# A gated linear attention and a maxout FFN: attention output computed with features on the rows, and smaller tiles for scores and state sums

## The chip, the cores and the metric

The kernel runs on one core of a Trainium2 chip. The metric is the device time of one execution in microseconds. Where a profile is quoted, its times are of one profiled execution: the span is the time from its first to its last instruction, and the execution's own time is a little longer. Engines are named as in the profile: PE (matrix products; PEld is its loading of the stationary operand), DVE, ACT and POOL (elementwise work), SP (issues transfers). Results of PE land in psum, which has eight banks here.

## What is computed

Four arrays q, k, v and alpha of 4 batches, 8 heads, 768 positions and 48 features. For each batch and head a 48 by 48 state runs over the positions, and its read-out goes through an FFN with a maximum over three products:

```
for t in range(S):
    state = alpha[:, :, t, :, None] * state + einsum('bhd,bhe->bhde', k[:, :, t], v[:, :, t])
    y[:, :, t] = einsum('bhd,bhde->bhe', q[:, :, t], state)
x = y.transpose(0, 2, 1, 3).reshape(B * S, H * D)              # 3072 x 384
out = max(max(x @ w1, x @ w2), x @ w3) @ w_out                 # 384 -> 768 -> 384
```

## The kernel before

**Groups and units.** The 768 positions of a batch are cut into chunks of 128. A group `n` is one batch and two neighbouring chunks, 256 positions, so there are 12 groups. On the 128 rows of the loaded tiles stand pairs of positions: rows 0 to 63 are chunk `i` = 0, rows 64 to 127 chunk `i` = 1, and the parity `r` of the position is an index beside the features. The eight heads of a group are two units `u` of four heads (`hh`); four heads are two pairs `j` of two heads `p`, and a pair of heads is padded to 2 x 64 features.

**Steps of a group.** The names are those of the steps in the code.

- `load`: transfers issued by SP. `aa`, `la` (POOL, DVE, ACT): products and logarithms of alpha. `Lp` (PE, L389), `L0` (DVE), `exp` (ACT, L398): prefix sums of the logarithms and their exponentials `ep` and `en`. `hp` (PE, L344), `e` and `G`: decays of whole chunks.
- `qk` (POOL or DVE, L403): q times `ep`, k times `en`, as 16-bit tiles. `v` (POOL or ACT): v scaled by `vsc`, a factor of the row.
- `tp` (PE, L421), `qkT` (DVE, L429): 16 transposes for a unit and their copy out of psum, so that features stand on the rows.
- `A` (PE, L441), `LA` (DVE, L449): scores of key against query, 16 matmuls for a unit with 48 rows by 64 stationary columns and 128 moving ones, and the causal mask. Keys stand on the rows of `LA`, queries in its columns.
- `pp` (PE, L472): state sums, k against v, for each chunk that a later one needs; 16 matmuls a group (8 in the last chunk pairs) with 64 rows by 128 stationary columns (two heads) and 96 moving ones. The off-diagonal blocks of the two heads are computed as well and not used. `add`, `Z`, `Zp` (DVE, POOL): the carried state, kept as a 16-bit tile `Z` with zero blocks between the heads.
- `yi` (PE, L509): output from the state, four matmuls a chunk with the queries `qkT` stationary, 128 by 128, and 96 columns of `Z` moving. `ya` (PE, L531): output from the chunk itself, 32 matmuls a group, `LA` stationary (64 by 128) and 48 columns of v moving, added to the same bank. The result `yp` has positions on the rows.
- `xb` (ACT or DVE, L247 and L249): `yp` out of psum, times `ysc`, a factor of the row. `xp` (PE, L551): three matmuls a chunk with `xb` stationary and a constant 0/1 matrix `order` moving, which put features on the rows and the positions back in their order. `xT` (DVE or ACT, L243): the copy out of psum.
- The FFN of a group: `gp` (PE, L575, six matmuls for each of six pieces of w2 - w1 and w3 - w1), `h0` and `h1` (ACT, DVE), `op` (PE, L603 and L606), `ob` (ACT, DVE) and `out` (SP). `d` (DVE, L281) makes the weight differences; `wt` and `mp` (L294, L307) make the product of w1 and w_out that carries the bypass.

**What sets the order.** Nothing is scheduled at run time. `ORDER` is a list written out ahead: each token is a step's number, the engine that runs it and the psum bank or banks that it gets (`17P0`: step 17 on PE with bank 0). `Plan.emit` (L100) issues the steps in that order, so every engine works through its own part of the list in order, and waits where a step needs another engine's result or a bank or tile that is still in use. Weights are loaded by transfers that POOL issues (L272) between its other work, activations by SP (L262).

Of the kernel before, what the change touches and what calls it, by code (L numbers as in the profile page):

```python
# [10 lines left out]
FP32 = mybir.dt.float32  # L11
# [7 lines left out]
CDEC = 0.92  # L19
# [7 lines left out]
6S 0S 3S 1S 2S 52S 5S 7S 8V 9A 4S 10A 11G 17P0 54S 18V 13A 53S 19A 14P1 98S 28P2 12A 20A 55S 29V  # L27
15A 22V 100S 30A 31A 21V 99S 56V 101S 24P3 16G 143S 58A 32V 145S 57A 33V 74P5 144S 59P6 25V 62P7
35P0 146S 23A 63V 205S 26P2 64A 36V 272S 65A 34A 206S 75V 37P0 67G 27V 207S 60A 40P47 77A 274S 76A
61G 339S 66V 208S 42V 78G 69P2 38V 273S 39G 79V 41V 73G 81P5 68A 102G 82V 70V 83P0 80G 104A 44P4  # L30
85G 84V 86P56 45P2 87V 71P0 88V 46A 119P3 72V 103A 47P5 90P2 49A 120V 91P4 122A 193P0 92V 95A 105P1
121A 89V 108P4 93P2 48A 43V 96P3 50P6 123V 51A 94A 124V 109V 126P5 111A 97A 195P7 189V 106A 187V
196A 262P2 127V 321P3 194A 188V 128P5 110A 113V 254P1 112G 129V 258P7 255A 130G 329P0 115P4 192V
330A 197P1 107G 116V 114A 125G 331P6 198A 190V 117P4 325P0 322A 118V 147G 148A 256P1 191V 149A
131P34 263A 257V 153P5 259A 264P2 154V 133V 326A 132V 164P1 260P7 156A 265V 327P0 165V 261V 167A
135P3 323P2 166A 332V 155A 136P7 324V 169G 201P1 140V 158G 150P6 199P5 202A 137A 157V 151A 168V
160P2 328V 171P6 203P1 159A 170G 172V 200A 161V 173P6 204A 175P05 209G 174V 162P2 333P1 211A 163V
276G 277A 210A 218P6 269P7 334A 152G 219V 539S 278A 176V 275S 134V 221A 340S 177V 220A 141P2 229P3
138P1 341S 285P4 222G 230V 179P0 139A 266P6 142V 406S 231A 286V 342S 232A 223V 288A 234G 279P1
180P2 270A 267V 287A 212P3 178V 392P7 181A 233V 213A 296P6 225P4 280A 215G 184A 297V 236P2 290G  # L40
394P1 226V 299A 298A 237V 301G 182P0 393A 388P4 183V 344A 185P5 343G 238P2 395V 224A 227P6 336P0
186A 228V 289G 235A 389A 214G 239V 217G 390P1 337A 216G 345A 292P5 338S 300G 240P74 473S 293V 363P0
352P2 396P3 408S 353V 241V 474S 354A 463P5 391V 397A 268S 242G 398P6 335S 291A 282G 243V 409S 461P7
464A 281G 364V 302G 407S 399V 366A 459P3 284G 271S 365A 244V 476S 245P1 355A 246P5 460V 307P60 671S
357G 247P 462V 605S 294P2 251A 465P4 283G 295V 248A 356G 252P7 411A 455P5 253A 308V 368G 457P1 456A
466V 249P2 359P6 410G 458V 250A 303P3 346P5 529P2 304V 310G 412A 525P1 360V 309G 347A 530A 367G
305P3 311V 369A 361P5 521P7 306V 526A 349G 350G 358A 312P2 523P0 351G 522A 362V 543G 313P1 413P3
419P4 430P7 314P 414A 431V 370P5 420V 433A 467P3 524V 315A 435G 371V 318A 421A 477G 372P0 422A
374P25 545A 470P6 436G 479A 375V 478A 348G 373V 376G 432A 379P4 434G 480P2 471A 403P7 468A 424V
377V 486P0 319P1 423G 404A 531P6 487V 378V 488A 405S 380P3 527P7 481A 532V 608S 320A 541S 489A 381P  # L50
609G 528V 544A 475S 426P1 437P5 382A 540S 415G 316P0 427V 503G 400P7 317A 438V 416G 385V 383P4
552P1 401V 386P2 384A 591P0 483V 387A 402S 553V 484G 428P5 672S 592A 439P3 675G 497P7 555A 655P2
440V 554A 425G 593P0 611A 485G 498V 589P1 500A 418V 429V 491G 546P3 499A 653P4 587P7 417G 654A 594V
441P56 547A 676A 490V 563P4 533P3 442V 588V 443G 444G 656V 661P0 534A 501G 564V 447P5 535S 663P7
590V 662A 606S 492G 677A 446P2 445V 657P3 674S 565A 502G 664V 542S 566A 493P0 448P 658V 472S 482G
556G 504P6 607S 494V 508P4 624A 469S 659P3 452A 449V 610A 618P0 505V 595P1 450P5 453P2 596V 597P6
451A 454A 509V 536P7 660V 511G 549G 619V 568G 598V 621A 506P1 495P4 620A 678P3 551G 537A 725P6 496V
569G 679A 538S 684P0 612P7 719P3 557G 673S 685V 507V 665P4 567G 550V 686A 629P5 695P1 548V 599P2
510V 613A 720A 681V 623V 666A 615V 683V 723P7 622G 696V 630V 698A 602P3 724V 631A 614G 558G 687A
726V 635A 688G 721P4 697A 600V 603A 512P7 700G 601S 513P0 722V 632A 625P1 667S 514P 604S 626V 699G  # L60
574P6 515A 559P3 570P1 518A 727P5 634G 571V 701A 519P7 575V 729P0 616G 728A 560V 577G 516P1 668P2
633G 517V 730V 520V 627P5 669A 572P3 689V 561P0 737P7 670S 617V 573V 731P2 738A 562V 741P7 732A
578P3 576V 745P4 742A 628V 690A 579P0 636P1 580P 637V 640P7 581A 691P5 584V 638P1 746A 582P3 692V
747P0 583A 641V 644P4 743P5 639V 642G 739P6 643G 680V 585P3 645P7 740V 702P1 586A 646P 682V 706P3
703V 647A 734P6 650A 748V 707V 744V 704P1 709G 693P3 759P7 708G 735V 694V 755P0 757P5 705V 711P6
752P3 710P4 761P1 753A 756A 754S 648P2 712P 760A 733S 651P3 649A 749P0 762V 652A 716V 713V 777P7
750A 763P2 751S 736S 717P1 714P3 781P6 718A 779P4 782V 765P0 715V 783P1 778V 799P6 764V 801P3 766V
800A 773P7 784V 775P2 758V 793P0 780V 797P6 774V 795P1 791P5 767P4 792V 802V 770P7 776V 768A 796V
769S 794V 785P5 798V 771V 803P3 786V 772S 787S 807P4 804P 808P 805V 788P2 809A 806S 810S 789A 790S
# [44 lines left out]
def kernel(  # L114
# [20 lines left out]
    DP = 64  # L135
    NP = H // 2
# [11 lines left out]
    rr = np.arange(P)  # L148
# [11 lines left out]
    d16_np = np.concatenate(  # L160
        [np.eye(P)] + masks + [turned[:, None] == rr[None, :]], axis=1).astype(np.float16)
    dec = CDEC ** (2.0 * pair - (HALF - 2.0))
    c32_np = np.stack(
        [np.concatenate([SIG / dec] * 2), np.concatenate([dec / SIG] * 2),
         np.full(P, HALF * np.log(CDEC))], axis=1
# [6 lines left out]
    d16 = sb.tile([P, 4 * P], FP16, name="d16")  # L172
    c32 = sb.tile([P, 3], FP32, name="c32")
    tri, hsel = c16[:, :P], c16[:, P:]
    ident, maskA, order = d16[:, :P], d16[:, P:3 * P], d16[:, 3 * P:]
    vsc, ysc, hbias = c32[:, 0:1], c32[:, 1:2], c32[:, 2:3]
# [16 lines left out]
    v16s = homes(NQ, [P, HH, 2, D], FP16, "v")  # L193
    qkTs = homes(NT_, [P, UB, 2, 2, P], FP16, "qkT")
    LAs = homes(NT_, [P, 2, 2, 2, P], FP16, "LA")
    xbs = homes(3, [P, DM], FP16, "xb")
# [16 lines left out]
    for t in qks:  # L213
        nc.vector.memset(t[:, :, :, :, D:], 0.0)
    for zz in Zs:
        for t in zz:
            nc.gpsimd.memset(t, 0.0)
# [20 lines left out]
    live = {}  # L238
    LEAD, SLOPE = 5.5, 1.9
    WAFTER = {2: (0,), 4: (1,), 7: (2,), 11: (3,)}  # L240
# [76 lines left out]
    def decay(n):  # L317
# [21 lines left out]
        key = ("hp", n)  # L339

        def totals(eng):
            live[key] = bank(key, [P, NP, 2 * UB], FP32)
            for j in range(NP):
                nc.tensor.matmul(live[key][:, j, :], la[:, 0, 2 * j:2 * j + 2, :], hsel,  # L344
                                 start=True, stop=True)

        plan.step("hp", "PE", 2 * n + 0.5, totals, banks=[key],
                  reads=[("la", n % 3, h, 0) for h in range(2)], writes=[key])
# [3 lines left out]
                                                   in_=live[key], func=AFT.Exp, bias=hbias,  # L352
# [27 lines left out]
    def prep(u):  # L380
# [4 lines left out]
        Lk, tk, Ak = ("Lp", u), ("tp", u), ("A", u)  # L385
# [5 lines left out]
        plan.step("Lp", "PE", u, cums, banks=[Lk], reads=[("la", n % 3, hh, 0)], writes=[Lk])  # L391
# [9 lines left out]
        for w, x, e in ((0, "q", ep), (1, "k", en)):  # L401
# [7 lines left out]
                  lambda eng: scaled(eng, v16, ld["v"][n % NL][:, hs], vsc),  # L409
                  reads=[("v", n % NL, hh)], writes=[("v16", u % NQ)])  # L410
        qkT, LA = qkTs[u % NT_], LAs[u % NT_]

        def trans(eng):
            live[tk] = banks2(tk, FP16)[:, :, :4 * P]
            for w in range(2):
                for j in range(2):
                    for r in range(2):
                        for i in range(UB):
                            rows = slice(i * HALF, (i + 1) * HALF)
                            at = (4 * w + 2 * j + r) * HALF  # L420
                            nc.tensor.transpose(live[tk][:, i, at:at + HALF],  # L421
                                                qk[rows, w, r, 2 * j:2 * j + 2, :],
                                                ident[rows, rows])

        plan.step("tp", "PE", u, trans, banks=[tk],
                  reads=[("qk", u % NQ, 0), ("qk", u % NQ, 1)],
                  writes=[tk])
        plan.step("qkT", "DVE", u,
                  lambda eng: nc.vector.tensor_copy(  # L429
                      out=qkT.rearrange("p i w j t -> p i (w j t)"), in_=live[tk]),  # L430
                  reads=[tk], writes=[("qkT", u % NT_)])

        def scores(eng):
            live[Ak] = banks2(Ak, FP32)
            for j in range(2):
                for r in range(2):
                    for i in range(UB):
# [237 lines left out]
```

## Time and profile before

| | us |
|---|---|
| median of 3 runs (151.91 to 154.11) | 153.44 |
| the profiled execution's own time | 153.0 |
| its span | 151.2 |
| first FFN matmul (L575) starts | 28.14 |
| last FFN matmul (L606) ends | 147.85 |

In a profile, "L441 PE MATMUL psum<-qkT 48*64 48x128 f16 x384" is the group of 384 matmuls of line 441 with a stationary tile of 48 rows by 64 columns and 128 moving columns. The chain of waits goes back from the last instruction to what released each; its pieces are given in order of time, with start and length in us, and a piece of PE lasts until the next begins. The slices are fortieths of the span, 3.78 us each, and their digits tenths of busy time. Matmuls are pipelined, so that the mean time of one in the groups (240 ns for L441) is its latency; what one costs is read from the lengths of whole pieces in the chain.

### The profile page before, as it was taken

Reading aid. Unit: us, or ns where it says so; the run is one execution under the profiler, and the core shown is the slowest. Engines: PE = TensorE matmul, PEld = TensorE weight load, DVE = VectorE, ACT = ScalarE, POOL = GpSimd, SP = SyncE. Lnnn points to the kernel's source line nnn. Section 1 sums busy time; section 2 is a strip of 40 time slices with the busy share of each in tenths; the row PEclk is TensorE's granted clock in tenths of the full one; section 3 lists DMA queues with packets and bytes.
Section 4 is the critical chain, followed back from the end, with each engine's and each line's share of the span. In section 5 each row is a group of like instructions: output and inputs, shape, how many; then the busy total and the mean of one; then the engine's idle time right before and its main releaser. Section 6 shows DMA issues by size and latency. Waiting matters only on the chain.

```text
span 151.2 us, 5265 instructions
## 1 busy us (share of the span) xinstructions
PE 133.5 (88%) x2220; PEld 102.4 (68%) x2220; DVE 120.7 (80%) x210; ACT 82.3 (54%) x185; POOL 69.3 (46%) x106
## 2 busy tenths in 40 slices
PE   0145498999999999999999999998999999999991
PEld 0133276677766778888677878766868877888660
DVE  3188988769999999999698998899899992395920
ACT  3467246829576996777967756536627305210111
POOL 8114920080390697798992865688800220000000
PEclk9999999999999999999999999999999999999999
DMA  5999999999999999999529929960410002300124
GB/s 127 273 261 261 266 213 211 240 249 221 279 260 262 262 252 261 282 310 270 114 59 259 290 60 259 255 191 0 160 56 0 4 4 81 127 4 0 52 104 156
DMA packets 55880, 26.45 MB, mean 175 GB/s; under 512 B 50737, under 2 KB 55857, under 8 KB 55857
## 3 DMA queue, kind: packets, MB, share of 16 engines
q1 hardware_dynamic: 53440, 23.60, 63.5%
q0 software_dynamic: 1984, 2.36, 9.0%
q8 instruction: 17, 0.28, 0.8%
q10 hardware_dynamic: 432, 0.17, 0.5%
q14 instruction: 7, 0.05, 0.1%
HBM read 23.76 MB, written 4.72 MB: 188 GB/s over the span
## 4 chain that ended last, share of the span: by engine, by line
PE 74%; DMA 11%; SPq 5%; DVE 3%; issue 3%; ACT 2%; POOL 1%; ACTq 0%; DVEq 0%; POOLq 0%
PE psum L575 31%; PE psum L606 14%; PE psum L603 7%; DMA wcat<-in_moe_w_dram 7%; SPq L262 5%; PE psum L441 4%; DMA qn<-in_q_dram 4%; PE psum L421 4%; PE psum L531 3%; PE psum L472 3%; PE psum L551 2%; PE psum L307 2%; PE psum L509 2%; PE psum L389 1%; DVE Z L373 1%
## 5 line engine op out<-in xcount | busy, mean ns | idle before, releaser
L575 PE MATMUL psum<-xT,wcat 128*128 128x256 f16 x432 | 55.3, 277 | 0.3 <-DVE wcat L281 0.3
L575 PEld LDWEIGHTS <-wcat 128*128 128x128 f16 x432 | 40.7, 99 | 6.6 <-DVE wcat L281 0.5
L449 DVE TENSOR_TENSOR LA<-psum,d 128x1024 f16<-128x1024 f32 x24 | 28.8, 1219 | 3.8 <-PE psum L441 2.6
L606 PE MATMUL psum<-wo,hT 128*128 128x384 f16 x144 | 27.3, 326 | 0.0
L591 DVE TENSOR_TENSOR hT<-psum,hT 128x512 f16<-128x512 f32 x36 | 23.8, 681 | 3.2 <-PE psum L531 2.8
L403 POOL TENSOR_TENSOR qk<-qn,ep 128x384 f16<-128x384 f32 x16 | 16.7, 1052 | 14.5 <-ACT ep L398 14.0
L243 ACT COPY ob<-psum 128x384 f32<-128x384 f32 x17 | 8.1, 484 | 24.7 <-PE psum L606 24.7
L403 POOL TENSOR_TENSOR qk<-kn,en 128x384 f16<-128x384 f32 x15 | 15.0, 1001 | 13.0 <-ACT en L398 8.5
L606 PEld LDWEIGHTS <-hT 128*128 128x128 f16 x144 | 14.1, 98 | 9.3
L584 ACT ACTIVATE hT<-psum 128x512 f16<-128x512 f32 x25 | 14.6, 600 | 8.1 <-PE psum L575 7.9
L429 DVE COPY qkT<-psum 128x1024 f16<-128x1024 f16 x24 | 16.0, 684 | 1.4 <-PE psum L421 1.1
L603 PE MATMUL psum<-past,xT 128*128 128x384 f16 x72 | 15.7, 327 | 0.0
L421 PE MATMUL psum<-d,qk 64*128 64x64 f16 x384 | 10.6, 200 | 5.2 <-DVE qk L403 4.0
L398 ACT ACTIVATE en<-psum 128x384 f32<-128x384 f32 x24 | 11.8, 496 | 5.3 <-DVE psum L393 4.1
L398 ACT ACTIVATE ep<-psum 128x384 f32<-128x384 f32 x24 | 11.7, 492 | 4.6 <-POOL qk L403 2.9
L373 POOL TENSOR_TENSOR Z<-U,G 48x192 f16<-48x192 f32 x12 | 6.0, 504 | 16.3 <-DVE U L486 15.8
L421 PEld LDWEIGHTS <-qk 64*128 64x128 f16 x384 | 8.1, 100 | 8.0 <-DVE qk L403 5.3
L243 ACT CAST xT<-psum 128x384 f16<-128x384 f32 x19 | 8.8, 483 | 6.0 <-PE psum L551 5.7
L324 POOL TENSOR_TENSOR aa<-an 128x384 f32<-128x384 f32 (+1 forms) x11 | 10.7, 972 | 2.6 <-DMA an<-in_alpha_dram 2.5
L247 ACT ACTIVATE xb<-psum,c 128x384 f16<-128x384 f32 x17 | 9.4, 580 | 4.2 <-PE psum L531 4.1
L586 DVE TENSOR_SCALAR hT<-psum 128x512 f16<-128x512 f32 x11 | 7.5, 686 | 4.4 <-PE psum L575 4.3
L247 ACT ACTIVATE v<-vn,c 128x384 f16<-128x384 f32 x14 | 8.6, 617 | 4.3 <-DMA vn<-in_v_dram 3.9
(54 smaller groups left out, 193.8 us busy)
## 6 DMA issues: line engine op xcount, KB each, us to landing
out_dram<-ob SPq DMA_DIRECT2D x24, 192.0 KB, 2.0
an<-in_alpha_dram SPq DMA_DIRECT2D x11, 384.0 KB, 6.1
kn<-in_k_dram SPq DMA_DIRECT2D x11, 384.0 KB, 5.9
qn<-in_q_dram SPq DMA_DIRECT2D x11, 384.0 KB, 6.5
vn<-in_v_dram SPq DMA_DIRECT2D x11, 384.0 KB, 6.1
wcat<-in_moe_w_dram POOLq DMA_DIRECT2D x2, 576.0 KB, 11.3
w1s<-in_moe_w_dram POOLq DMA_DIRECT2D x1, 576.0 KB, 8.0
wo<-in_moe_w_out_dram POOLq DMA_DIRECT2D x1, 576.0 KB, 7.6
```

The costliest lines, as they stand in the source:

```text
L243: (nc.scalar.copy if eng == "ACT" else nc.vector.tensor_copy)(out=out, in_=in_)
L247: nc.scalar.activation(out=out, in_=in_, func=AFT.Copy, scale=factor)
L398: lambda eng, t=t, sign=sign: nc.scalar.activation(out=t, in_=live[Lk], func=AFT.Exp, scale=sign),
L403: lambda eng, w=w, x=x, e=e: on[eng].tensor_mul(qk[:, w, :, :, :D].rearrange("p r h d -> p h r d"), ld[x][n % NL][:, hs], e),
L421: nc.tensor.transpose(live[tk][:, i, at:at + HALF], qk[rows, w, r, 2 * j:2 * j + 2, :], ident[rows, rows])
L429: lambda eng: nc.vector.tensor_copy(out=qkT.rearrange("p i w j t -> p i (w j t)"), in_=live[tk]),
L449: lambda eng: nc.vector.tensor_mul(LA.rearrange("p a j r t -> p (a j) (r t)"), live[Ak].rearrange("p a (j t) -> p (a j) t", j=2), maskA.un ...
L575: nc.tensor.matmul(live[gk][:, jj, :], wcat[:, kt, g, c0:c0 + P], xT[:, kt, :], start=(kt == 0), stop=(kt == NFT - 1))
L584: nc.scalar.activation(out=h, in_=live[gk], func=AFT.Relu)
L591: lambda eng, h=h, gk=gk: nc.vector.tensor_max(h, live[gk], h),
L603: nc.tensor.matmul(live[ok], xT[:, kt, i * P:(i + 1) * P], past[:, kt, :], start=(kt == 0), stop=False)
L606: nc.tensor.matmul(live[ok], hT[:, kt, i * P:(i + 1) * P], wo16[:, kt, :], start=False, stop=(kt == NJ - 1))
```

## The change

The output of attention is computed with features on the rows at once. The 384 features of a position are twelve pieces of 32; piece `f` goes to rows 32 * (f mod 4) and column block f // 4 of the bank, which is how `xT` has them.

- `yi`: pieces of 32 features of `Z` are stationary (128 by 32), the queries `qkT` move (128 columns); 12 matmuls a chunk for 4.
- `ya`: 32 features of v are stationary (64 by 32), the masked scores `LA` move (128 columns); 64 matmuls a group for 32. A piece of 32 features can span two heads, and then gets a product from each; for that v16 is padded to 64 features with zeros, by six POOL memsets at the start.
- `xb` and `xp` go, with the matrix `order` and the tiles `xb`. `xT` is now one DVE product for a chunk, out of psum, times `ysc`, which has become a factor of the column (a 128 by 128 constant); it also puts the two parities back in order, by an output with a stride of two elements.
- `A`: 32 matmuls a unit with 32 stationary columns for 16 with 64. `pp`: stationary pieces of 32 features of one head, and only that head's 48 columns of v moving; 64 (32) matmuls for 16 (8).
- Eight matmuls with a zero tile, one to each bank, open the program on PE.
- Steps change their numbers, and `ORDER` is a new list: engines and order of other steps differ too. Of the `qk` products 36 are on POOL and 12 on DVE (31 and 17 before), of the `Z` products 28 on POOL and 4 on DVE, not counting the 8 of `Zp` (23 and 9 before); `h0` is on ACT 27 times and on DVE 9 (25 and 11); `xT` is on DVE 24 times (5, and 19 on ACT). Two further modes (`merged`, `joined`) come with the code and are switched off (`TB, HB = 99, 99`).

At the start the new list has these orders (loads by array and group; 0a and 0b are the two halves of group 0):

```
SP before:   k0b a0a a0b q0a k0a a1 q0b v0b v0a k1 q1 a2 v1 k2 q2 v2 a3 k3 q3
SP after:    a0b a0a k0a q0a q0b a1 k0b v0a v0b a2 q1 k1 q2 v1 k2 a3 v2 q3 k3
POOL before: aa G qk(unit 2, k) G qk(unit 3, q) w1 w2 aa v w3 qk(unit 4, q) w_out
POOL after:  aa aa G G v aa qk(unit 2, q) qk(unit 3, q) w1 w2 w3 qk(unit 4, k) G qk(unit 4, q) qk(unit 5, q) qk(unit 5, k) w_out
PE before, ahead of the first gp: ... pp(1) ya(0) A(2) Lp xp yi(1) ya(1) wt hp Lp xp xp xp tp(5) wt
PE after, ahead of the first gp:  ... ya(0) A(3) pp(1) tp(4) A(2) yi(1) tp(5) wt ya(1) wt A(5) wt A(4) Lp
DVE before, ahead of d: ... LA(2) L0 xb add add qk(5) qk(5) L0
DVE after, ahead of d:  ... add xT(0) xT(0) LA(2) qkT(5) qkT(4) xT(1) xT(1)
```

The diff, without the order list, the two modes that are switched off, and the declarations (`QD`, `AW` and `KW` are 32):

```diff
+    for t in v16s:
+        nc.gpsimd.memset(t[:, :, :, D:], 0.0)
...
         def scores(eng):
...
-                    for i in range(UB):
+                    for s0 in range(0, P, AW):
                         for p in range(2):
-                            rows = slice(p * DP, p * DP + D)
-                            at = (2 * j + r) * P
-                            nc.tensor.matmul(
-                                live[Ak][i * HALF:(i + 1) * HALF, p, at:at + P],
-                                qkT[rows, i, 1, j, r * HALF:(r + 1) * HALF],
-                                qkT[rows, i, 0, j, :], start=True, stop=True)
+                            i, rows = s0 // HALF, slice(p * DP, p * DP + D)
+                            at, of = (2 * j + r) * P, r * HALF + s0 % HALF
+                            nc.tensor.matmul(live[Ak][s0:s0 + AW, p, at:at + P],
+                                             qkT[rows, i, 1, j, of:of + AW],
+                                             qkT[rows, i, 0, j, :], start=True, stop=True)
...
         def sums(eng):
...
-                        for i in range(n_i):
-                            rows = slice(i * HALF, (i + 1) * HALF)
-                            nc.tensor.matmul(live[keys[i]][:, 2 * hh + j, :],
-                                             qk[rows, 1, r, 2 * j:2 * j + 2, :],
-                                             v16[rows, 2 * j:2 * j + 2, r, :],
-                                             start=(r == 0), stop=(r == 1))
+                        for d0 in range(0, P, KW):
+                            for i in range(n_i):
+                                rows = slice(i * HALF, (i + 1) * HALF)
+                                heads = qk[rows, 1, r, 2 * j:2 * j + 2, :]
+                                own = slice(0, 2) if KW == P else slice(d0 // DP, d0 // DP + 1)
+                                nc.tensor.matmul(
+                                    live[keys[i]][d0:d0 + KW, 2 * hh + j,
+                                                  own.start * D:own.stop * D],
+                                    heads.rearrange("p h d -> p (h d)")[:, d0:d0 + KW],
+                                    v16[rows, r, 2 * j + own.start:2 * j + own.stop, :D],
+                                    start=(r == 0), stop=(r == 1))
...
+        def rows_of(i, f):
+            t, at = divmod(f, 4)
+            return live[keys[i]][at * QD:(at + 1) * QD, t, :]
         def inter(i):
...
+            for c in range(3):
+                for j in range(NP):
+                    f = 4 * c + j
+                    pair, q_ = divmod(f, 3)
+                    nc.tensor.matmul(rows_of(i, f),
+                                     Zs[i][b][:, pair, q_ * QD:(q_ + 1) * QD],
+                                     qkTs[us[pair // 2] % NT_][:, i, 0, pair % 2, :],
+                                     start=c == 0, stop=False, skip_group_check=True)
...
+        def intra():
...
+            for p, q_ in ((0, 0), (0, 1), (1, 1), (1, 2)):
+                for r in range(2):
+                    for pair in range(NP):
                         for i in range(UB):
+                            f = 3 * pair + q_
+                            hh, j = divmod(pair, 2)
                             rows = slice(i * HALF, (i + 1) * HALF)
+                            vf = v16s[us[hh] % NQ].rearrange("p r h d -> p r (h d)")
+                            c0 = (2 * j + p) * DP + q_ * QD - p * D
+                            nc.tensor.matmul(rows_of(i, f), vf[rows, r, c0:c0 + QD],
+                                             LAs[us[hh] % NT_][rows, p, j, r, :],
+                                             start=(i, f % 4) not in begun, stop=False,
+                                             skip_group_check=True)
...
-            plan.step("xb", "ACT DVE", rank,
...
-            plan.step("xp", "PE", rank, turn, banks=[xk], reads=[("xb", m % 3)], writes=[xk])
...
+            to = xTs[n][:, :, i * P:(i + 1) * P].rearrange("p t (s r) -> p t r s", r=2)
+            plan.step("xT", "DVE", rank,
+                      lambda eng, to=to, yk=yk: nc.vector.tensor_mul(
+                          to, live[yk].rearrange("p t (r s) -> p t r s", r=2),
+                          ysc.rearrange("p (r s) -> p r s", r=2).unsqueeze(1).broadcast_to(
+                              [P, NFT, 2, HALF])),
+                      reads=[yk], writes=[("xT", n, i)])
...
+            zero = Zs[0][0].rearrange("p j d -> p (j d)")
+            for row in range(NBANKS):
+                nc.tensor.matmul(psall[:, row, :DM], zero[:, :P], zero, start=True, stop=True)
```

## The prediction

> **What bounds the kernel now.** I read the page's busy shares and slices first, then the chain of waits in order of time, then the groups by line and shape, last the DMA packets of the start. The page:
>
> ```profile
> PE 133.5 (88%) x2220; PEld 102.4 (68%) x2220; DVE 120.7 (80%) x210; ACT 82.3 (54%) x185; POOL 69.3 (46%) x106
> PE   0145498999999999999999999998999999999991
> DVE  3188988769999999999698998899899992395920
> q8 instruction: 17, 0.28, 0.8%
> ```
>
> From slice 8 (28 us) to the end PE is full, and DVE is nearly so until slice 34 (130 us). ACT and POOL have room. The chain (start, length, what) shows what fills PE:
>
> ```profile
> 16.76 10.67 DMA wcat<-in_moe_w_dram
> 27.53 0.57 DVE wcat L281
> 28.14 2.74 PE psum L575 x12
> ...
> 56.96 0.66 PE psum L575 x6
> 57.61 0.34 PE psum L421 x16
> ...
> 61.84 0.34 PE psum L509 x8
> 62.18 0.45 PE psum L472 x16
> 62.63 0.40 PE psum L531 x32
> 63.03 0.37 PE psum L441 x16
> 63.40 0.76 PE psum L575 x6
> 64.16 0.17 PE psum L551 x3
> ...
> 92.13 0.34 PE psum L472 x8
> 92.46 0.76 PE psum L575 x6
> ...
> 110.32 0.80 PE psum L441 x48
> ```
>
> The first FFN product waits for a weight (w2, landed 27.43) and its subtraction; from 28.14 to 147.85 PE hands the chain from piece to piece. So the end is 28.14 plus PE's own time, and PE's time is what I price:
>
> - A full-array matmul takes about 2.7 ns + 0.417 ns a column: 56 ns for 128 columns (L551, 0.17/3), 42.5 for 96 (L509, 0.34/8), 109 for 256 (L575, 0.66/6). Twelve at the start took 228 ns (2.74/12): PE is at half speed until about 31 us.
> - Pieces of the array run at once. L441 also moves 128 columns, and costs (0.80 - 0.10)/48 = 14.5 ns: four 64 by 64 tiles share one 56 ns slot. L531 costs 12.5 ns: two tiles share a slot of 25. L472 with both chunks costs 21 (two in 42.5), with one chunk 42.5 (0.34/8).
> - Each change of tile shape costs 0.095 us: six L575 take 0.66 after a full-array matmul and 0.76 after a 64-row one.
>
> **The change, part by part, from the first FFN matmul on.** I counted the steps behind that point in both instruction orders.
>
> 1. Turning products (L551) go: 60 of the 72 stand there, 60 x 56 = -3.35 us. The other 12 lay before 28 us.
> 2. State sums, 10 steps. Before: 16 matmuls in 8 slots of 42.5, or 8 in 8 slots, so 3.4 us. After: 64 (or 32) matmuls of 48 columns, eight (four) tiles at once, still 8 slots. No row shows 32-column tiles. Lower bound of a slot: 25 ns (L531, 48 columns); upper: 56 (L441, as if loading the narrow weights set the slot). 2.0 to 4.5 us; I take 2.0, since L531 loads the same 128 weight columns per half of the rows in 25 ns. -1.4, up to +1.1.
> 3. Output within the chunk, 10 steps: 32 matmuls in 16 slots of 25 become 64 in 8 slots of 56: 4.03 to 4.47, +0.45. Upper bound, if only four tiles run at once as in L441: 16 slots of 56, +4.9.
> 4. Output from the state, 18 steps: 4 slots of 42.5 become 12 matmuls in 3 slots of 56: 0. Upper bound (no sharing across columns): 12 x 56, +9; but L441 shares two column halves already, so at most 6 slots, +3.
> 5. Scores: 16 matmuls in 4 slots of 56 become 32 in 4 slots: 0 a step. Upper bound 8 slots, +4.0 for 18 steps. Behind the first FFN matmul stand 18 steps and not 20: -0.45, paid earlier (8).
> 6. One transposition step, one weight transposition and one prefix sum also move ahead of it: -0.65.
> 7. Shape changes behind that point: 59 before, 61 after: +0.2. (Scores, sums and output now share a shape, but state outputs no longer share the FFN's.) Bounds 0 and 0.2, as the row prices them.
>
> Sum on PE: -3.35 - 1.4 + 0.45 - 0.45 - 0.65 + 0.2 = -5.2 us.
>
> 8. The start. w1 and w2 (the first two weights) are issued on POOL behind both q products of group 1 instead of one, q's load being the last to arrive in both orders with the same 2304 KB ahead of it: one product of 1.05 us less the 0.2 us G that stood between, so the weight lands 0.65 to 1 later, 28.1 to 28.4. The rest of the chain is longer. On SP, group 2's k goes from 14th to 15th load and the k of group 1 from 10th to 12th; by the packets of before the 15th ends at 20.3 us, and its word comes 1.35 later. Then POOL makes four products of group 2 (4.2, to about 25.5 us); transposition, a weight transposition and group 1's output follow on a cold PE (about 2.5, to 28.0), two xT on DVE (1.1), ahead of which the subtraction no longer stands, and then it (0.57): 29.7. PE meanwhile does two weight transpositions and scores 5 and 4 ahead of the FFN, cold, to 30.1. I take the first FFN matmul at 30.1, +2.0; bounds +0.7 (weight alone) and +3.
> 9. PE is then dense from about 25.6 on, so most of the half-speed stretch behind 28.14 (12 x 119 ns = 1.4 us) has passed: -0.8, bounds -1.4 and 0.
> 10. DVE loses 7 xb (608 ns), 5 xT (551), 5 qk (about 600), 5 Z (about 530), 2 relu (686), and gains 0.6 in small ones: -13.4. It gains 24 xT. Nearest row: L486, 128x384 out of psum, 548 ns; upper, L403 on DVE with turned output, 647. So 13.2 to 15.5: 0 to +2 on an engine that stands idle 30 us of the span. From the first subtraction to the last masked score its rows sum to 98 us in both orders, and before they took 97.5 us of wall. At the same filling the last mask would come at 127.2 and the PE work behind it (17 us) would end at 144.1, which is where PE alone would put it. I take 0, bounds 0 and +3.
> 11. ACT loses 36 instructions and gains two: 18 us less, not bound. POOL gains 5 qk (1.03), 5 Z (0.5), 6 memsets: +8, 77 of 149 us; its waits (15.8 us for U, 14.0 for ep) cover it. The six memsets and the eight opening products (8 x 0.32 us at half speed) lie under the load wait, since POOL had none of it until 6.14 us and PE until 5.2; without that cover, 1 us. The larger constant (1.5 to 65 KB, another shrinks by 32) lies behind the one that PE waits for first: 0.
> 12. PE has 1344 more pairs of instructions: 11 more fetches of 256. A fetch takes 1.14 us by its row; a dense run of scores, sums and output would use 256 instructions in about 0.9. 0 to 3 us; I take 0: before, fetches came at least 4.4 us apart and no PE wait stands there.
>
> Total: -5.2 + 2.0 - 0.8 = -4.0. The profiled execution took 153.0 us (span 151.2, 1.8 around it; median 153.44): **149.0 us**. Its last 3.4 us (ob, output transfer) stay.
>
> **The rivals.**
>
> *Instructions, not columns, set PE's pace (slower).* The densest row is L531, a pair of weight load and matmul each 12.5 ns; the forecast needs 7 (scores, output) and 3.3 (sums). If 12.5 is all the queue gives, a score step takes 0.40 and not 0.22 (18: +3.2), an output step 0.80 and not 0.45 (10: +3.5), sums 0.80 or 0.40 and not 0.2 (+4.3): +11, 160 us. It decides from about 8.5 ns a pair on (scores +0.9, output +1.0, sums +2.2). For it: no row is denser. Against: the slots of L531 and L441 are full by columns or by the 25 ns, and inside a slot L441's matmuls start 3.3 ns apart. The upper bounds of 3 to 5, part of them, and a fetch that is late end here too: 154 to 161. Chance 0.20.
>
> *Every matmul takes a slot of 25 ns, in whichever tile.* L344, 4 columns, takes 25 each, so the slot is there. Scores would take 0.80 a step, output 1.6, sums 1.6: +32, 181 us. But L531's 32 in 0.40 us are already twice as fast. Chance 0.02. [...]
>
> *DVE takes PE's place, or the start slips.* xT can now run on DVE alone, behind masks of 1.2 us. With xT at 0.65 and the start at +3 the gain is 1 to 2.5: 150.5 to 152. For it: DVE has some 8 us of slack in 97.5. Against: the way from output to FFN loses two copies. Chance 0.20.
>
> *More of the early work fits below the weight wait.* First FFN matmul at 28.8, all of it warm: 147 or less. Chance 0.05.
>
> [...]
>
> **How the numbers follow.** Forecast 0.53 (146.5 to 151), DVE or start 0.20, instruction pace 0.20, slot of 25 ns 0.02, better than forecast 0.05. The range 146.5 to 157 leaves out the 25 ns slot, the worse half of the instruction pace (0.10) and what lies below (0.04). About 2% is what a measurement of this kernel can tell from no change. Against the median, faster by over 2% is below 150.4: nearly all of the forecast's case and the better one, 0.55. Within 2% (to 156.5): the DVE case, the forecast's edge, a mild instruction pace, 0.27. Slower: 0.18.
>
> **What would show it.** Right: in the chain after, a score step of 32 near 0.23 us (0.32 with a shape change), an output step of 64 near 0.45, a sum step of 64 near 0.21; first FFN matmul near 30; no DVE releaser with over 2 us in PE's waits behind it. Wrong: score steps of 0.4, sums of 0.45 or more, PE idle for xT, or a first FFN matmul past 31.

## The result, and the profile after

| | before | after |
|---|---|---|
| median, us | 153.51 (151.91 to 154.11, 4 runs) | 176.98 (175.79 to 177.74, 4 runs) |
| profiled execution, us | 153.0 | 177.68 |
| its span, us | 151.2 | 175.9 |
| pairs on PE (load of a stationary tile, matmul) | 2220 | 3564 |
| first FFN matmul starts, us | 28.14 | 38.18 |

The changed kernel is slower: the ratio of the times is 1.154, with a 95% interval of 1.142 to 1.166. The forecast was 149.0, its range 146.5 to 157.0. Medians and ratios, here and below, leave out the slow runs, those over 1.5% above the fastest of their kernel.

The page of the changed kernel, the lines that answer to those shown of before, and the granted clock:

```profile
PE 140.3 (80%) x3564; PEld 103.8 (59%) x3564; DVE 119.4 (68%) x210; ACT 68.1 (39%) x151; POOL 76.2 (43%) x122
PE   5254725849999969829967989999978959999992
DVE  2377818535988867914966879797979539739901
PEclk9999999999999999996999999999999999999999
q8 instruction: 28, 0.46, 1.1%
PE 73%; issue 13%; SPq 7%; DMA 4%; ACT 1%; DVE 1%; DVEq 0%
```

PE's row was nearly all nines from slice 7 on; now it has holes (slices 8, 14, 17, 20 and 21, 32, counted from 0). No other engine fills them: DVE's row has holes beside them. The last line, the chain by engine, says what stands there: 13% "issue", time in which the engine waited for nothing that the profile shows. Next the chain in order of time, three of its stretches (start, length, what; L482 scores, L515 state sums, L585 output in the chunk, L294 weight transpositions, L621 first FFN products):

```profile
20.68 0.32 PE psum L515 x20
21.00 3.87 issue
24.88 0.57 PE psum L515 x28
...
29.31 0.24 PE psum L585 x4
29.54 1.53 issue
31.07 1.01 PE psum L585 x50
...
34.15 0.54 PE psum L482 x25
34.69 3.13 issue
...
38.39 3.22 PE psum L621 x18
...
55.36 0.67 PE psum L482 x64
...
59.24 0.61 PE psum L515 x64
...
73.78 0.18 PE psum L515 x19
73.96 4.17 issue
78.13 0.51 PE psum L515 x42
78.64 2.67 PE psum L621 x12
```

The waits stand inside steps. The 64 sums at 73.78 had all that they need, since they are one step with one set of operands; PE ran some twenty, stood still for 4.17 us and ran the rest. PE's waits by what ended them (us in total, times, longest) name no engine either:

```profile
PE psum L482 <- issue: 5.9, 3, 3.1
PE psum L585 <- issue: 5.3, 4, 2.0
PE psum L515 <- issue: 4.9, 2, 4.2
PE psum L442 <- issue: 1.5, 2, 1.0
```

What they have in common shows when PE's instructions (loads, matmuls and the five waits among them) are numbered from 0 by their start in the trace. The 13 gaps of over 0.5 us between starts that no other engine's result explains, and the packet of the instruction queue (q8) that came last before each:

```
gap at us   length   line   number on PE          packet of q8 ended
  20.79      4.09    L515    705 =  2*256 + 193     23.64
  29.26      1.81    L585    961 =  3*256 + 193     29.76
  34.38      3.44    L482   1217 =  4*256 + 193     36.19
  52.51      0.68    L442   1729
  61.73      1.66    L585   2241
  67.33      0.60    L402   2497
  73.77      4.36    L515   3009                    76.69
  90.70      2.56    L482   3777                    91.80
 101.95      0.95    L515   4289
 113.61      0.55    L585   4801
 129.99      1.16    L442   5569
 133.93      0.67    L482   5825
 142.26      2.17    L585   6337 = 24*256 + 193    142.93
                     sum 24.7 us
```

Every one stands ahead of a number that leaves 193 when divided by 256, and PE goes on 1.2 to 1.6 us after the end of a packet of 16 KB (q8: 28 packets, 0.46 MB), one for each 256 instructions. So PE runs out of instructions. Of the 24.7 us, 9.3 lie ahead of the first FFN matmul and 15.4 behind it. In the trace of before no gap at such an edge exceeds 0.2 us; the shortest stretch from one edge to the next took 5.1 us there.

### The profile page after: what moved, and what is told of

It is laid out like the page before. It is cut to its first block, busy times and chain, and to the rows that moved or that the text cites. A ratio compares the mean times of both kernels' runs of the same rounds, so it can differ in the third digit from the quotient of the medians.

```text
span 175.9 us, 7917 instructions
## 1 busy us (share of the span) xinstructions
PE 140.3 (80%) x3564; PEld 103.8 (59%) x3564; DVE 119.4 (68%) x210; ACT 68.1 (39%) x151; POOL 76.2 (43%) x122
## 4 chain that ended last, share of the span: by engine, by line
PE 73%; issue 13%; SPq 7%; DMA 4%; ACT 1%; DVE 1%; DVEq 0%
PE psum L621 29%; PE psum L652 13%; PE psum L649 7%; SPq L262 7%; PE psum L482 5%; PE psum L585 5%; DMA vn<-in_v_dram 4%; PE psum L442 4%; PE psum L515 3%; PE psum L559 3%; PE psum L307 2%; PE psum L294 1%; PE psum L402 1%; ACT v L247 1%; PE psum L349 1%
## 5 line engine op out<-in xcount | busy, mean ns | idle before, releaser
L621 PE MATMUL psum<-xT,wcat 128*128 128x256 f16 x432 | 54.6, 282 | 0.0
L621 PEld LDWEIGHTS <-wcat 128*128 128x128 f16 x432 | 42.2, 101 | 7.1
L421 POOL TENSOR_TENSOR qk<-qn,ep 128x384 f16<-128x384 f32 x20 | 19.9, 999 | 19.7 <-ACT ep L416 16.1
L421 POOL TENSOR_TENSOR qk<-kn,en 128x384 f16<-128x384 f32 x16 | 16.3, 1016 | 6.9 <-ACT en L416 5.2
L599 DVE TENSOR_TENSOR xT<-psum,c 128x384 f16<-128x384 f32 x24 | 13.2, 582 | 8.4 <-PE psum L585 8.4
L482 PE MATMUL psum<-qkT 48*32 48x128 f16 x768 | 12.1, 241 | 6.9 <-issue 5.9
L515 PE MATMUL psum<-v,qk 64*32 64x48 f16 x640 | 7.8, 192 | 9.9 <-issue 8.8
L585 PE MATMUL psum<-LA,v 64*32 64x128 f16 x768 | 10.3, 235 | 5.3 <-issue 5.3
L442 PE MATMUL psum<-d,qk 64*128 64x64 f16 x384 | 10.2, 202 | 5.0 <-DVE qk L421 3.1
L482 PEld LDWEIGHTS <-qkT 48*32 48x32 f16 x768 | 8.0, 96 | 9.6 <-issue 8.7
L411 DVE TENSOR_TENSOR psum<-psum,la 128x192 f32<-128x192 f32 x24 | 8.3, 359 | 7.7 <-PE psum L402 7.6
L515 PEld LDWEIGHTS <-qk 64*32 64x32 f16 x640 | 6.4, 91 | 11.7 <-issue 11.0
```

Of the source, the lines that this page charges most:

```text
L421: lambda eng, w=w, x=x, e=e: on[eng].tensor_mul(qk[:, w, :, :, :D].rearrange("p r h d -> p h r d"), ld[x][n % NL][:, hs], e),
L442: nc.tensor.transpose(live["tp", v][d0:d0 + TW, i, at:at + HALF], heads.rearrange("p h d -> p (h d)")[:, d0:d0 + TW], ident[rows, rows])
L482: nc.tensor.matmul(live[Ak][s0:s0 + AW, p, at:at + P], qkT[rows, i, 1, j, of:of + AW], qkT[rows, i, 0, j, :], start=True, stop=True)
L515: nc.tensor.matmul(live[keys[i]][d0:d0 + KW, 2 * hh + j, own.start * D:own.stop * D], heads.rearrange("p h d -> p (h d)")[:, d0:d0 + KW], ...
L585: nc.tensor.matmul(rows_of(i, f), vf[rows, r, c0:c0 + QD], LAs[us[hh] % NT_][rows, p, j, r, :], start=(i, f % 4) not in begun, stop=False, ...
L621: nc.tensor.matmul(live[gk][:, jj, :], wcat[:, kt, g, c0:c0 + P], xT[:, kt, :], start=(kt == 0), stop=(kt == NFT - 1))
```

## The experiments

The theory: PE's instructions come in blocks of 256, and the next block is asked for only when the last one is entered; where the work of a block is shorter than that fetch, PE waits. Rivals: narrow tiles cost time themselves; each further instruction or fetch costs a fixed time; the new order of loads and steps is the cause.

**The edges shifted.** The changed kernel, with 64 small pairs more behind the opening products:

```diff
+            for _ in range(64):
+                nc.tensor.matmul(psall[:, 0, :4], zero[:, :P], zero[:, :4], start=True, stop=True)
```

> The changed kernel with 64 more matmuls of 4 columns (128 instructions of PE) behind the opening products, where PE waits for loads anyway. Theory 1 (instruction fetch: PE's instructions come in blocks of 256, only one block ahead, and a dense stretch uses a block up before the next has come): waits that no semaphore explains stay at the same place in the count, every 256 instructions, at number 193 modulo 256 of all PE instructions, and so 64 matmuls earlier in the work than before; none stays at its old matmul. One more fetch at most (28 or 29). Time 170 to 184 us, since other places of the work now meet a block's edge. Theory 2 (the narrow tiles: something in the 64 by 32 products themselves, bank, tile or queue, makes PE halt): the waits stay at the same matmuls of the same lines as in the changed kernel, and the time within 1% of 177.

Measured: 173.33 us in one run, 3.6 less than the changed kernel's median though it has more to do. Nine gaps of over 0.3 us, together 14.6 us, all ahead of a number that leaves 193; but other matmuls stand there now. The step of sums that had stood still for 4.17 us runs through, and the wait has gone into the wide FFN products behind it (the chain):

```profile
71.21 0.60 PE psum L585 x55
71.81 0.60 PE psum L515 x61
72.41 1.42 PE psum L621 x12
73.82 0.08 PE psum L402
73.91 0.98 PE psum L621 x9
74.89 2.14 issue
77.03 0.49 PE psum L621 x3
```

A wait that moves by instruction number, and into a 128 by 128 tile, is none of the narrow tile's own. A fixed price for each instruction falls too, since 128 more instructions took 3.6 us away. The waits at edges do not count one for one, though: they fell by 10.1 us and the time by 3.6. Behind the first FFN matmul 2.7 us of waits for DVE and ACT came in, and the clock was granted at half for 3.4 us more than in the changed kernel.

**One part at a time.** The changed kernel with scores in 64 by 64 tiles and sums in 128 columns, so that the output part and the new order remain:

```diff
-    TW, AW, KW = 128, 32, 32
+    TW, AW, KW = 128, 64, 128
```

> The changed kernel with scores in 64 by 64 tiles and sums in 64 by 128 tiles again: 2700 matmuls instead of 3564, output and xT as changed. Theory 1 (fetch): 21 or 22 fetches, waits only at 193 modulo 256, and far fewer, together 3 to 10 us instead of 24; time 152 to 161. Theory 2 (narrow tiles): waits inside the output steps, which hold 1008 of the 2416 narrow matmuls; about 10 of the 24 us stay, 163. Theory 3 (DVE is late with xT): 170 or more, since all of xT stays on DVE.

Measured: 160.47 us in one run (three more took 163.45, 163.49, which is the profiled one, and 227.84), before 153.27 beside it. 2692 pairs, and gaps at block edges of 3.3 us only, of which 2.0 lie inside an output step, not the 10 of theory 2. So at least some 4 us have another cause. The chain of its start:

```profile
15.58 16.07 DMA an<-in_alpha_dram
31.64 0.08 issue
31.73 0.99 POOL aa L324
32.72 0.02 issue
32.74 0.53 ACT la L334
33.27 0.04 issue
33.32 0.32 PE psum L402
33.63 0.43 PE psum L621 x2
```

The first FFN product stands on PE behind the prefix sum (`Lp`, L402) of group 3. That needs group 3's alpha, issued at 15.58 and landed at 31.64, while the weight difference for the FFN was there at about 29.1. This is a cost of the new order; what it is worth is tested further down.

The other half: the kernel before, in its own order, with scores and sums in 64 by 32 tiles (the two loops of the diff above) and the eight opening products.

> The kernel before with scores and sums in 64 by 32 tiles alone (and the eight opening products): 3092 matmuls, output, turning products and xT as before, the order of the kernel before. Theory 1 (fetch): 24 or 25 fetches; unexplained waits at one place modulo 256, 8 to 18 us together; time 160 to 173. Theory 2 (narrow tiles): 1408 of 2416 narrow matmuls, about 14 us, 167, waits inside scores and sums and at no fixed place in the count. Theory 3 (DVE): within 2% of before, since DVE has nothing new.

Measured: 165.45 us in one run, with 3092 pairs. First FFN matmul at 31.38. PE's waits:

```profile
PE psum L441 <- issue: 3.4, 1, 3.4
PE psum L578 <- issue: 2.5, 1, 2.5
PE psum L474 <- issue: 1.9, 1, 1.9
```

All three end at numbers that leave 193 (8.5 us between starts), one of them inside FFN products (L578). What the rest of the loss is was not taken apart. Alone, the halves cost 7.2 and 12.2 us, together 23.5.

**The fetch by itself.** Not the computation (its output is zeros): the 48 loads, and beside them 5120 matmuls of four columns in eight 64 by 32 tiles, which wait for nothing.

```diff
+        for _ in range(PAIRS // 8):
+            for j in range(4):
+                for i in range(2):
+                    rows = slice(64 * i, 64 * i + 64)
+                    nc.tensor.matmul(psall[32 * j:32 * j + 32, i, :4], Z[rows, :32], Z[rows, :4],
+                                     start=True, stop=True)
```

> Not the computation: 5120 matmuls of 4 columns in eight 64 by 32 tiles (10240 instructions, 40 blocks) that wait for nothing, beside the 48 loads of 384 KB that the kernel makes, all issued at once; the output is zeros. Theory 1 (fetch): PE advances in blocks of 256 with a wait at each edge; a block takes 4.5 to 7 us while the loads run (some 75 to 90 us), 3.3 to 3.7 after, so 150 to 200 us in all; within a block the instructions go at 4.2 ns each (1.07 us a block). Theory 2 (no fetch limit): 10240 instructions at 4.2 ns, PE done after 43 us with no steps in it, and the loads end the kernel at about 80 us.

Measured: 172.8 us in one run. Its page and its group of matmuls, PE's waits, and PE's timeline once the loads were done:

```profile
PE 47.1 (28%) x5120; PEld 43.8 (26%) x5120; DVE 0.5 (0%) x2; POOL 0.4 (0%) x5
q8 instruction: 39, 0.64, 1.5%
```

```profile
PE psum L54 <- issue: 106.9, 39, 3.9
```

```profile
85.13 1.18 PE L54 MATMUL psum<-Z 64*32 64x4 f16 x128 [2.55 <-issue]
88.59 1.18 PE L54 MATMUL psum<-Z 64*32 64x4 f16 x128 [2.28 <-issue]
92.04 1.18 PE L54 MATMUL psum<-Z 64*32 64x4 f16 x128 [2.28 <-issue]
```

39 waits at 39 edges, 128 pairs between any two. A block takes 1.0 us to run and 3.45 from start to start. From the third block to about 70 us, beside the loads, it is 4.0 to 4.55; behind that 3.45 to 4.0. With no other work in the kernel, nothing but the fetch can be waited for. The packet itself (about 1 us) is a third of it: behind the loads it starts about 1.1 us after the block is entered (1.6 to 2.3 beside them), and PE goes on some 1.4 us after its end. In the changed kernel, while its loads ran (208 to 278 GB/s in slices 1 to 16), packets started up to 4.2 us after the edge, and blocks that waited took 4.2 to 6.7 us (31.07 to 37.82 is the longest). In the shifted kernel one short block, with wide products ahead of it, did not wait: it took 1.75 us (137.03 to 138.77), and its packet had started at 136.29, before PE came to the block.

**As many instructions, spread.** The kernel before, in its own order and tiles, each FFN matmul cut into pieces of 128 moving columns. The pieces of one bank are begun in turns, by which part of the sums is lost, so that its output isn't the reference's; the work is the same.

```diff
-    nc.tensor.matmul(live[gk][:, jj, :], wcat[:, kt, g, c0:c0 + P], xT[:, kt, :], ...)
+    for h0 in range(0, TG, P):
+        nc.tensor.matmul(live[gk][:, jj, h0:h0 + P], wcat[:, kt, g, c0:c0 + P],
+                         xT[:, kt, h0:h0 + P], ...)
```

> The kernel before, its own order and tiles, with every FFN matmul cut along its moving columns into pieces of 128 (256 into two, 384 into three): 864 more pairs of instructions, 3084 in all, as many as the kernel with scores and sums in narrow tiles (3092, 165.45 us), but spread over the wide products, where a block of 256 instructions takes 5 to 7 us. By its columns it costs 432 times 3 ns and 216 times 6 ns: 2.6 us. Theory 1 (only a block shorter than the 3.5 to 6.7 us that a fetch needs makes PE wait): 155 to 157 us, waits at block edges 1 us in all. Rival (the number of instructions or of fetches costs as such, whatever stands between them): 864 pairs at 14 ns each, 165 us, as in the kernel with as many pairs.

Measured: 154.29 us (153.7 to 155.73, 3 of 4 runs; before 152.66), ratio to before 1.016 (1.004 to 1.027). The profiled execution is the fourth, of 157.16 us, and still has little to show behind 28 us (2.0 us between starts, at three edges):

```profile
PE psum L576 <- issue: 0.7, 2, 0.4
PE psum L606 <- issue: 0.6, 1, 0.6
```

So 3084 pairs cost 1.6 us here and 3092 cost 12.2 above. The number of instructions and of fetches alone does not decide; how many stand close together does. (These pieces are also wide where those tiles were narrow; that the tile is not the cause rests on the shifted edges.)

**The new order.** The output part alone once more, with `Lp` and `hp` of group 3 put behind five FFN products on PE:

```diff
-109P0 136A 141P5 178A ... 234P2 302A 138P3 142V 297P0 139A 121V 305P1 152P4
+109P0 136A 178A ... 234P2 302A 297P0 121V 305P1 141P5 138P3 142V 139A 152P4
```

> The output part alone (scores in 64 by 64 tiles, sums in 128 columns), in the new order, but with two prefix sums and one chunk decay of group 3 (Lp 6, hp 3 and the L0 behind) put behind five FFN products on PE instead of ahead of the first. Theory 1 (the new order makes PE wait for group 3's alpha load, which landed at 31.64 us in the run with the output part alone, ahead of a first FFN product whose weight had been ready since about 29.1): the first FFN matmul starts at 29 to 30 us instead of 33.6, and the time falls by 3.5 to 5 us, from 163.5 to 158.5 to 160; waits ahead of matmuls of number 193 modulo 256 stay at 2 to 6 us in all. Rival (the start does not matter, since DVE or a later transfer sets the end): the first FFN matmul comes early, but the end stays within 1.5 us of 163.5.

Measured: 161.81 us (161.52 to 163.1, 4 runs): the expectation was missed, and against the 160.47 of the output part alone nothing was gained. The first FFN product did come early (29.64), but the second step then waited 4.0 us for a copy on ACT. The same kernel with sums in 64 by 64 tiles (`KW = 64`) shows it:

> As the kernel with the prefix sum put later, and the state sums in 64 by 64 tiles besides (two matmuls of 48 columns for each of 96): 160 more pairs of instructions, 1.25 more fetches. By slots alone a step of 32 takes eight slots of 25 ns and not 42.5: 1.4 us less than that kernel. Theory 1 (instructions arrive in blocks of 256, the next at least 3.5 us after the last): the saving is partly or wholly lost where a block gets denser, so between 1.4 us less and 2 us more than that kernel. Rival (narrow tiles cost by themselves, about 24 us for the 1344 pairs of the whole change, 18 ns a pair): 3 us more.

Measured: 159.43 us (159.16 to 160.77, 3 of 4 runs), 2860 pairs, and one gap of 1.64 us at an edge. That is 2.4 us less than the last kernel, 1.0 beyond what was expected; with more instructions it had fewer waits at edges (4.0 us there), since its edges fell elsewhere. ACT's timeline, and then the chain:

```profile
32.69 0.52 ACT L334 ACTIVATE la<-aa 128x384 f16<-128x384 f32 x1 [5.42 <-POOL aa L324]
33.12 0.78 ACT L243 COPY w1T<-psum 128x768 f16<-128x768 f16 x1
```

```profile
15.44 16.14 DMA an<-in_alpha_dram
...
33.95 5.28 PE psum L621 x24
```

The copy (`w1T`), whose input had been ready since about 29.5, stands on ACT behind the logarithm `la` of group 3, and holds the bank of the next product. So the load reached PE on a second way, through another engine's queue; and behind the wait 24 products took 220 ns each where 109 is usual. The two logarithms put behind two relus on ACT, and the next alpha load of SP with them:

```diff
-181P4 137A 120P6 ... 109P0 136A 178A 441S 318S ... 234P2 302A 297P0
+181P4 120P6 ... 109P0 178A 318S ... 234P2 302A 137A 136A 441S 297P0
```

> The kernel with the output part, scores and sums in 64 by 64 tiles and the prefix sum of group 3 put later, with the two logarithms of group 3 (la on ACT) also put behind the first two relus there, and the next alpha load of SP behind them. In the run before, the second FFN product waited 3.4 us for a copy of a weight transposition (w1T) that stood on ACT behind those logarithms, and they behind group 3's alpha load (landed 31.59), and the 24 products after it took 5.28 us, about half of it the lower granted clock. Theory (the wait for that load is the rest of the start's cost, and the clock follows it): the second product no longer waits, the first FFN matmul of the full stretch starts at 29.5 to 30.5, PE is at full clock from there, and the time falls by 4 to 6 us from 160.1 to 154 to 156, within 2% of the kernel before. Rival (behind the start DVE sets the end, or blocks of instructions get denser and wait): less than 2 us of it are left, 158 to 160.

Measured: 154.59 us (154.12 to 155.14, 4 of 6 runs; before 152.69), ratio to before 1.011 (1.0065 to 1.0154): 4.8 us back, as expected. The products behind the start take 114 ns each:

```profile
34.26 4.09 PE psum L621 x36
```

What is left: three gaps at edges, 3.0 us in all. The longest, 1.8 us, is also a wait of the sums for an `xT` on DVE, as the gap of 1.64 us in the run before was; the chain:

```profile
119.91 1.64 DVE xT L599 x3
121.55 0.57 issue
122.12 0.43 PE psum L515 x16
```

`xT` held the sums until 121.55. The packet for this edge ended at 120.74, and PE went on 1.38 us after it, within the 1.2 to 1.6 us seen above. So both stood in the way, and the fetch ended last. The same order with the whole change (tiles 32 wide):

> The whole change (all tiles 32 wide) with the same order as the kernel with the logarithms put later. Theory 1: there the blocks of instructions and not the alpha load hold up the first FFN matmul (waits of 4.09, 1.81 and 3.44 us at block edges stood ahead of it), so the order alone gives back 0 to 3 us of 177: 174 to 177.5, with waits at numbers 193 modulo 256 of 18 us or more in all. Rival (the order is the main cost of the whole change too): 168 to 171.

Measured: 180.23 us in one run, outside both expectations on the upper side. Gaps at edges sum to 22.9 us; the first FFN matmul stands at 37.82 (38.18 in the changed kernel), and 30 products behind it took 6.25 us instead of 3.3. So in this run of the whole change the waits at block edges cover the load, and the order is worth nothing. Why it is 3 us above the changed kernel is open; its clock was granted at half for 10.2 us of PE's work, that of the changed kernel for 3.4.

**Sums alone.** The kernel before with its sums in 64 by 64 tiles and the opening products.

```diff
-    nc.tensor.matmul(live[keys[i]][:, 2 * hh + j, :], qk[rows, 1, r, 2 * j:2 * j + 2, :],
-                     v16[rows, 2 * j:2 * j + 2, r, :], ...)
+ for d0 in range(0, P, DP):
...
+    nc.tensor.matmul(live[keys[i]][d0:d0 + DP, 2 * hh + j, h * D:(h + 1) * D],
+                     heads.rearrange("p h d -> p (h d)")[:, d0:d0 + DP], v16[rows, 2 * j + h, r, :], ...)
```

> The kernel before, its own order, with the state sums alone in 64 by 64 tiles, and the eight opening products: 160 + 8 more pairs of instructions. In that kernel no block of 256 instructions took under 5.1 us, so theory 1 leaves every wait at a block edge below 0.3 us, and the slots of 25 ns instead of 42.5 save up to 1.4 us: 151.5 to 153, against 153.4. Rival (each pair more costs 18 ns as in the whole change): 156.5.

Measured: 152.95 us (152.16 to 154.02, 12 runs; before 152.66), ratio 1.004 (0.9996 to 1.0084): no difference. No gap at an edge over 0.3 us. A step of 32 took 0.37 us in the chain where one of 16 had taken 0.45, 0.08 less and not the 0.14 that slots give. No version here beats the kernel before.

## Why the prediction was wrong

**The step that failed is 12, the fetches.** Their number was right (28 packets for 17). Their price was not: "0 to 3 us; I take 0", and the runs show 24.7 us of waits at block edges. That the profiled executions also lie 24.7 us apart is in part chance, since the waits do not count one for one and PE's own work went wrong too (below). Two errors made it. The row of the queue gives the packet's own time, 1.14 us, and I read it as the time of a fetch; from the entry of a block to the next one it is 3.45 to 4.55 from the third block on where PE does nothing but wait for it, and up to 6.7 in the changed kernel. And the bound of 3 us had no row. The text had both that were needed: fetches "came at least 4.4 us apart" (4.2 in the trace, packets at 70.07 and 74.27), and a dense block runs in 0.9. No row showed a fetch that came sooner, so each dense block could cost 3.5 us, eleven of them 38. The mechanism was named, as a late fetch, but as a tail of 154 to 161 to the rival that instructions set the pace. That rival had the right side, with a chance of 0.20, and 16 us too little. In all the profiled execution came 28.7 us behind the forecast: 8.1 at the start, 14.3 in gaps behind it (15.4, 1.1 before) and 6.4 in PE's own time (steps 1 to 7 and 9).

**PE's work (1 to 7), forecast -5.2.** From the first FFN matmul on, PE's time without gaps of over 0.3 us went from 118.6 to 119.0 us, 5.6 more than forecast. Half speed behind waits is 2.6 us of the 119.0 (18 products in 3.22 us, 1.97 usual; 12 in 2.67, 1.31 usual, where PEclk is 6), against 1.4 behind 28.14 before: 1.2 us more, where step 9 had forecast 0.8 less, an estimate from that one stretch of before. The rest is pace. In a step of 64 sums (59.24) the first 32 started within 0.12 us, as forecast, and behind a pause of 0.10 a pair came every 8.33 ns: 0.61 us for the 0.21 of the forecast. Two score steps in a row took 0.67, and 56 matmuls of the output 0.62. The threshold that the rival gave, 8.5 ns a pair, was almost met; its 12.5 was not. For state outputs (step 4) the sharing of columns was right: 24 took 0.45 to 0.58 with a change of shape, for 0.34 by slots plus 0.1.

**The start (8), forecast 30.1, measured 38.18.** 9.3 us of block waits stand ahead of it. Without them it would still have been missed: with fewer instructions it came to 33.4, since I followed the weight, the group 2 products and their output, but not `Lp` of group 3, which the list of orders at the start shows as the last step ahead of the first `gp`. Behind it on PE stood the FFN, behind its logarithm on ACT the copy `w1T`.

**DVE, ACT and POOL (10, 11)** went as forecast: `xT` took 582 ns (548 to 647 forecast), POOL 76.2 us (77), ACT 14 us less (18). DVE was not the bound: its longest idle time, 8.7 us ahead of the masks, ended with PE's scores. With fewer instructions the rival has one place, the sums behind an `xT`, where a fetch ended as late.

**The slot of 25 ns** (before, the matmuls of L344 start 25 ns apart) fell as argued: in the step of 64 sums 32 matmuls of 48 columns started within 0.12 us, with 32 loads of 32 columns inside the same time. So the upper bound of step 2, 56 ns for a slot of sums, was not reached there either: 32 matmuls in eight tiles are four slots, 224 ns at that price.

## What to carry to other kernels

Before an edit adds small matmuls, number PE's instructions and look at how long each stretch of 256 (128 pairs) takes: here a stretch with under 3.5 us of work waited unless wide products stood just ahead of it, and beside a full load queue up to 5.2 us of work still waited. Put narrow work in pieces between wide work, or leave it in larger tiles: 864 more pairs cost 1.6 us where they stood among wide products, and 872 cost 12.2 where they stood together. And when a written order changes, follow on every engine what now stands ahead of the first critical step, back to the latest load.

## What the runs showed of the hardware

- **Instructions came to PE in blocks of 256, one block ahead.** Every wait at an edge stands at a number that leaves 193 modulo 256, with 256 instructions from edge to edge and one packet of 16 KB for each. In the kernel that only fetches, the packet of the next block starts about 1.1 us after a block is entered (1.6 to 2.3 beside the loads), and a block is stretched to 3.45 to 4.0 us when no loads run and, from the third on, to 4.0 to 4.55 beside the loads. In the changed kernel it is up to 6.7, and the waits come to 24.7 us. Before, where the shortest block took 5.1 us, no gap at an edge exceeds 0.2 us.
- **The first 32 pairs of a step started faster than the rest.** In a step of 64 pairs of eight tiles (59.24 in the changed kernel), 32 pairs start at 3.3 ns inside their slots, then one comes every 8.33 ns, 4.17 ns an instruction; in the kernel that only fetches, 128 pairs take 1.0 us by the same two rates. From this I estimate that PE has up to 64 instructions in hand ahead of the one it runs. That would also explain the block of 1.75 us that did not wait: by it a block is entered up to 64 instructions before PE gets to it, and its successor is asked for the earlier, the longer these take. No run tested this, but it fits: in the twelve traces no packet started less than 0.97 us, and no next block less than 3.45 us, after the start of the instruction 64 ahead of an edge, and five of the 17 packets before started 0.4 to 1.5 us ahead of PE's passing the edge.
- **Behind some waits PE also worked at half speed.** Behind the wait of 4.17 us, 12 products took 222 ns each for 109 (PEclk 6); in the kernel with the logarithms put later, where the wait for the copy is gone, 36 took 4.09 us, 114 ns each. PEclk does not always show it: the first twelve FFN products from 38.18 on took 213 ns each, in slices where it is 9.
